# Chunked attention and a gated feed-forward on one core: q and k turned by the DMA crossbar from unit 8 on, and a new order around the first two blocks

## The chip, the core and the metric

The kernel runs on one core of a Trainium2 chip. The metric is device time in microseconds (us), the median of several executions. An execution has five engines that matter here: PE (TensorE: matmuls into PSUM), ACT (ScalarE), DVE (VectorE), POOL (GpSimd, which here issues loads and little else) and SP (SyncE, which issues stores and DMA transposes). DMAs that change the type are issued from POOL; every engine's own instructions run in the order in which the program emits them.

## The reference

```python
q, k, v: (8, 8, 576, 64) float32      # batch, heads, sequence, head size
# attention within chunks of 64 tokens, 9 chunks per sequence
scores = (1 / sqrt(64)) * q_c @ k_c^T           # 64 x 64 for a chunk and head
attn   = softmax(scores, axis=-1)
x      = (attn @ v_c)  -> (4608 tokens, 512)     # heads side by side
h      = x @ w_in                                # 512 -> 2048
g      = h * sigmoid(beta * h)
out    = g @ w_out                               # 2048 -> 512, float32
```

## The kernel before

All matmuls run in fp16 and sum in fp32. The 4608 tokens are cut into 18 **units** of 256 tokens (four chunks), and two units make a **block** of 512 tokens; there are nine blocks, `j` = 0 to 8.

A unit is attended in these steps, each a function that emits its instructions at once:

- `load_qk(u)`, `load_v(i)`: casting DMAs from POOL. Four units of q and k are held (`qk` pool, `bufs=4`); v stays as a whole. A partition of the q tile holds two neighbouring tokens, so a run of q in memory is 512 bytes.
- `emit_T(u)`: two DVE stream transposes (line 135) of k and q, on pairs of fp16 values taken as fp32 in 32 x 32 blocks. Head size lies then on 32 partitions, in an even and an odd half `e`. It ends with `loads_to(u + 4)`, which puts the loads of a unit four further on POOL's queue.
- `emit_sc(u)`: the scores (line 187), 64 matmuls with 32 rows and 64 columns of PE: 8 heads, 2 halves that accumulate, 4 chunks. ACT takes the exponential of all into `et` (line 196).
- `emit_pv(u)`: attention times v (line 208), 32 matmuls with 64 rows and 64 columns and 65 columns streamed; the 65th column, ones, gives the softmax's sum.
- `emit_norm(u, s)`: DVE's reciprocal and product, for one half (128 tokens) of the unit (lines 218, 220).
- the turn of x for the next matmul: `emit_xt_pe` (four PE transposes into `xp`, line 235, and a copy on ACT, line 237) in units 0 to 3 and 5, `emit_xt_dma` (a DMA transpose from SP, line 243) in the others.

The feed-forward of a block is `emit_m(j, m)` for 16 values of m (first layer: 4 matmuls at line 254 into `hps`, a tanh on ACT at line 262 and a product on DVE at line 263, which gives `gt`; it can run on half of the columns), and `emit_t(j, t)` for four groups of 128 tokens (second layer: 16 matmuls at line 276, a scaled copy `osb` on ACT at line 286 and a store from SP). Sigmoid is written through tanh, with the halves in `beta2` and in the last copy. `hps`, `ops`, `xp` and `warm` share four PSUM buffers; scores and one of the two PV results share one more (`ps_s`).

The order is written out by hand, and each engine keeps it. At the start, q and k of unit 0 come in two halves of four heads as fp32, four DMAs on SP's queue (line 301), and are cast by ACT (line 150) and DVE (line 151) in `emit_T_half`. Idle matmuls (`emit_idle`) stand between the steps. Then unit 1 is attended while the first layer of block 0 begins on its first 256 columns, and after it the second layer of block 0 runs, with the attention of unit 2 in it. For block 1 and later, each step gets a place between 0 and 1 in the block, and all are sorted by it: `m` and `h` (an `m` on columns 256 to 511) are first-layer steps of block j, `t` is a half of a second-layer group of block j - 1, and `att_items(u, a0, w)` places the attention of unit u from `a0` on over a width `w`:

```python
return [(a0, 2, ("sc", u)), (a0 + 0.40 * w, 3, ("pv", u)),
        (a0 + 0.41 * w, 3, ("norm", u, 0)), (a0 + 0.55 * w, 3, ("norm", u, 1)),
        (a0 + 0.70 * w, 3, ("T", u + 1))]
```

Block 1 (`j == 1`) has only first-layer steps, with the attention of unit 4 and the scores of unit 5 in it; the second layer of block 0 is over by then. From block 3 on, a block holds 16 first-layer steps, 8 second-layer halves and the attention of the two units of the next block.

Of the kernel before, what the change touches and what calls it, by code (L numbers as in the profile page):

```python
# [8 lines left out]
FP32 = mybir.dt.float32  # L9
# [6 lines left out]
def kernel(  # L16
# [10 lines left out]
    nc = tc.nc  # L27
# [27 lines left out]
    ident = const.tile([128, 128], FP16)  # L55
    idle = const.tile([128, 512], FP16)
    HH = H // 2
    raw0 = [[const.tile([128, HH, 2, D], FP32, name=f"raw{i}{a}") for i in range(2)] for a in range(2)]
    qk0 = [[const.tile([128, HH, 2, D], FP16, name=f"h0{i}{a}") for i in range(2)] for a in range(2)]
    qkT0 = [[const.tile([128, HH, CH, 2], FP16, name=f"t0{i}{a}") for i in range(2)] for a in range(2)]  # L60
    braw = const.tile([128, 32], FP32)
# [5 lines left out]

    blocks = [(u, 2) for u in range(0, NU, 2)]
    NB = len(blocks)
    unit_block = {}  # L70
    for j, (u0, n) in enumerate(blocks):
        for u in range(u0, u0 + n):
# [13 lines left out]
    def load_qk(u):  # L86
        for src, dst, nm in ((q, q_t, "qu"), (k, k_t, "ku")):
            t = qk_p.tile([128, H, 2, D], FP16, tag=nm, name=nm)
            for off, n, b, s in runs(u * UNIT, UNIT):
                nc.gpsimd.dma_start(  # L90
                    out=t[off // 2:(off + n) // 2],
                    in_=src[b, :, s:s + n, :].rearrange("h (p r) d -> p h r d", r=2),
                )
            dst[u] = t
# [35 lines left out]
    def emit_T(u, which=("kT", "qT")):  # L130
        for nm in which:
            src, dst = {"kT": (k_t, kT), "qT": (q_t, qT)}[nm]
            a = src.pop(u)
            t = qt_p.tile([128, H, CH, 2], FP16, tag=nm, name=nm)
            nc.vector.transpose(  # L135
                out=t.rearrange("p h s e -> p (h s e)").bitcast(FP32).rearrange(
                    "p (h i r) -> p h r i", h=H, r=2),
                in_=a.rearrange("p h r d -> p (h r d)").bitcast(FP32).rearrange(
                    "p (h r i) -> p h r i", h=H, r=2),
            )  # L140
            dst[u] = t
        loads_to(u + 4)

    et_t = {}
# [2 lines left out]
    xt_t = {}  # L147

    def emit_T_half(a):
        nc.scalar.copy(out=qk0[a][0], in_=raw0[a][0])  # L150
        nc.vector.tensor_copy(out=qk0[a][1], in_=raw0[a][1])
        for i in (0, 1):
            nc.vector.transpose(
                out=qkT0[a][i].rearrange("p h s e -> p (h s e)").bitcast(FP32).rearrange(
                    "p (h i r) -> p h r i", h=HH, r=2),
                in_=qk0[a][i].rearrange("p h r d -> p (h r d)").bitcast(FP32).rearrange(
                    "p (h r i) -> p h r i", h=HH, r=2),
            )
# [21 lines left out]
    def emit_sc(u, split=False):  # L180
        qt, kt = qT.pop(u), kT.pop(u)
        sc = ps_s.tile([128, 2, H, CH], FP32, tag="s", name="sc")
        for h in range(H):
            for e in range(2):
                for c in range(4):
                    p0, o0 = 32 * c, 64 * (c % 2)
                    nc.tensor.matmul(  # L187
                        out=sc[o0:o0 + 64, c // 2, h, :],
                        lhsT=kt[p0:p0 + 32, h, :, e],
                        rhs=qt[p0:p0 + 32, h, :, e],  # L190
                        start=(e == 0),
                        stop=(e == 1),
                    )
        et = et_p.tile([128, 2, H, CH], FP16, tag="et", name="et")
        for s in ([0, 1] if split else [slice(0, 2)]):
            nc.scalar.activation(out=et[:, s], in_=sc[:, s], func=ACTF.Exp, scale=scale)  # L196
        et_t[u] = et

    def emit_pv(u):
        et = et_t.pop(u)  # L200
        for s in range(2):
            i = 2 * u + s
            pool, tag = ((ps_x, "x"), (ps_s, "s"))[s]
            x = pool.tile([128, 2, 4, 128], FP32, tag=tag, name="x")
            for g in range(4):
                for r in range(2):
                    for c in range(2):
                        nc.tensor.matmul(  # L208
                            out=x[64 * c:64 * c + 64, r, g, 0:D + 1],
                            lhsT=et[64 * r:64 * r + 64, s, 4 * c + g, :],  # L210
                            rhs=vbig[64 * r:64 * r + 64, i, 4 * c + g, 0:D + 1],
                        )
            x_t[u, s] = x

    def emit_norm(u, s):
        x = x_t.pop((u, s))
        rd = rd_p.tile([128, 2, 4, 1], FP32, tag="rd", name="rd")
        nc.vector.reciprocal(out=rd, in_=x[:, :, :, D:D + 1])  # L218
        x16 = x_p.tile([128, 2, 4, D], FP16, tag="x16", name="x16")
        nc.vector.tensor_tensor(  # L220
            out=x16, in0=x[:, :, :, 0:D], in1=rd.to_broadcast([128, 2, 4, D]), op=ALU.mult
        )
        x16_t[u, s] = x16

    def xt_at(u, s):
# [5 lines left out]
    def emit_xt_pe(u, s, on_act=True):  # L231
        xf = x16_t.pop((u, s)).rearrange("p r h d -> p (r h d)")
        xp = ps_p.tile([128, 4, 128], FP16, tag="p", name="xp")
        for g in range(4):
            nc.tensor.transpose(out=xp[:, g, :], in_=xf[:, g * 128:(g + 1) * 128], identity=ident)  # L235
        if on_act:
            nc.scalar.copy(out=xt_at(u, s), in_=xp)  # L237
        else:
            nc.vector.tensor_copy(out=xt_at(u, s), in_=xp)

    def emit_xt_dma(u, s):
        xf = x16_t.pop((u, s)).rearrange("p r h d -> p (r h d)")
# [52 lines left out]
    with tc.manual_schedule():  # L295
        nc.vector.memset(idle, 0.0)
        nc.vector.memset(braw, 0.0)  # L297
        nc.vector.memset(vbig[:, :, :, D:D + 1], 1.0)
        for a in range(2):
            for i, src in enumerate((q, k)):  # L300
                nc.sync.dma_start(  # L301
                    out=raw0[a][i],
                    in_=src[0, HH * a:HH * a + HH, 0:UNIT, :].rearrange("h (p r) d -> p h r d", r=2),
                )
        bv = moe_beta.rearrange("(m w f) -> w m f", w=4, f=32)
# [52 lines left out]
        for s in range(4):  # L358
            for t in range(4):
                if s == 2 and t == 1:  # L360
                    emit_T(2)
                if s == 2 and t == 3:
                    emit_sc(2)
                if s == 3 and t == 0:
                    emit_pv(2)
                    emit_norm(2, 0)
                    emit_norm(2, 1)
                if s == 3 and t == 2:
                    emit_xt_pe(2, 0)
                    emit_xt_pe(2, 1)  # L370
                emit_t(0, t, 4 * s, 4 * s + 4)
        emit_T(3)
        emit_m(1, 0, 0, 256)
        emit_m(1, 1, 0, 256)
        emit_sc(3, True)
        for m in range(2, 5):
            emit_m(1, m, 0, 256)
        emit_pv(3)
        emit_norm(3, 0)
        emit_norm(3, 1)  # L380
        for m in range(5, 10):
            emit_m(1, m, 0, 256)
        emit_xt_pe(3, 0)
        emit_m(1, 10, 0, 256)
        emit_xt_pe(3, 1)

        def att_items(u, a0, w):
            return [(a0, 2, ("sc", u)), (a0 + 0.40 * w, 3, ("pv", u)),
                    (a0 + 0.41 * w, 3, ("norm", u, 0)), (a0 + 0.55 * w, 3, ("norm", u, 1)),
                    (a0 + 0.70 * w, 3, ("T", u + 1))]  # L390

        for j in range(1, NB):
            items = []
            if j == 1:
                items += [(0.04 * m, 0, ("h", m)) for m in range(11)]
                items += [(0.44 + 0.11 * (m - 11), 0, ("m", m)) for m in range(11, KFF)]
                items += [(0.05, 3, ("T", 4)), (0.25, 2, ("sc", 4)), (0.42, 3, ("pv", 4)),
                          (0.43, 3, ("norm", 4, 0)), (0.50, 3, ("norm", 4, 1)), (0.58, 3, ("T", 5)),
                          (0.85, 3, ("sc", 5))]
            else:  # L400
                m0 = 0.27 if j == 2 else 0.02
                items += [(m0 + (1 - m0) * m / KFF, 0, ("m", m)) for m in range(KFF)]
                for t in range(4):
                    for hf in range(2):
                        items.append((0.98 * (t + 0.5 * hf) / 4, 1, ("t", t, hf)))
                if j == 2:
                    items += [(0.01, 3, ("pv", 5)), (0.02, 3, ("norm", 5, 0)), (0.06, 3, ("norm", 5, 1)),
                              (0.13, 3, ("xp", 5, 0)), (0.19, 3, ("xp", 5, 1)), (0.20, 3, ("T", 6))]
                if j + 1 < NB:
                    if j == 2:  # L410
                        items += att_items(6, 0.32, 0.34) + att_items(7, 0.66, 0.30)
                    else:
                        for i in range(2):
                            items += att_items(2 * j + 2 + i, 0.03 + 0.43 * i, 0.43)
            items.sort(key=lambda it: it[:2])
            for _, _, it in items:
# [68 lines left out]
```

## Time and profile before

| | |
|---|---|
| time, median of 4 runs | 300.25 us (299.41 to 301.15) |
| the profiled execution | 300.13 us |
| its span, first to last instruction | 298.4 us |
| mean granted TensorE clock | 0.988 |
| PE, DVE, ACT busy | 282.4, 152.1, 148.5 us |
| PE alone on the chain that ended last | 88% |
| DMA transposes, casting loads of q, k, v | 26 of 128 x 512 fp16; 68, most of 128 or 256 KB as written |

The span is what the profile shows of one execution, and the time of that execution is 1.7 us longer. "Busy" is the union of an engine's instructions; a busy PE need not be a PE at its peak. A view by stage tells more than the totals: the same engine can be full in one stage and waiting in another. Times within the profile are counted from the span's start. "Landing" of a DMA is counted from its issue.

### The profile page before, as it was taken

To read this page: it belongs to the slowest core of one execution; us is meant where nothing else is said; L and a number is where in the kernel's file an instruction comes from. 1 tells how busy PE (TensorE), PEld (TensorE's weight loads), DVE (VectorE), ACT (ScalarE), POOL (GpSimd) and SP (SyncE) were. 2 spreads that over 40 slices of the span, in tenths; PEclk is the share of its full clock that TensorE was granted. 3 is DMA by queue.
4 is the path that set the end of the run, shared out by engine and by line. 5 is a ranking of instruction groups with operands and counts; after the bars stand their busy time and mean duration, and the time that the engine had idled before them with its cause. 6 is when DMAs were issued, how large, how long until landed. Compare 5 with 4: busy or idle time off the path is not lost.

```text
span 298.4 us, 7145 instructions
## 1 busy us (share of the span) xinstructions
PE 282.4 (95%) x3046; PEld 142.1 (48%) x3046; DVE 152.1 (51%) x278; ACT 148.5 (50%) x232; POOL 78.9 (26%) x104
## 2 busy tenths in 40 slices
PE   6679999787999999999999999999999999999995
PEld 2555445663544444444444444444444444444444
DVE  2557514787446738373737373737273736443300
ACT  3278417774645555445544554545555454544411
POOL 8663478384406041431153104000000000000000
PEclk9599999999999999999999999999999999999999
DMA  8999999999986992939292929211120112100011
GB/s 151 180 194 204 163 178 208 210 165 161 164 99 100 130 141 74 142 76 140 73 139 76 142 64 147 73 37 51 57 73 28 47 57 74 45 37 35 35 73 71
DMA packets 101136, 32.20 MB, mean 108 GB/s; under 512 B 88176, under 2 KB 96624, under 8 KB 101104
## 3 DMA queue, kind: packets, MB, share of 16 engines
q0 software_dynamic: 79392, 17.83, 65.5%
q1 hardware_dynamic: 21568, 13.78, 15.5%
q8 instruction: 24, 0.39, 0.5%
q10 hardware_dynamic: 144, 0.13, 0.1%
q14 instruction: 8, 0.07, 0.1%
HBM read 36.71 MB, written 9.44 MB: 155 GB/s over the span
## 4 chain that ended last, share of the span: by engine, by line
PE 88%; DVE 5%; DMA 2%; ACT 2%; issue 1%; SPq 0%; DVEq 0%; ACTq 0%
PE ops L276 41%; PE hps L254 39%; PE sc L187 4%; DMA raw<-in_k_dram 2%; PE x L208 2%; DVE gt L263 2%; DVE x L220 1%; PE ops L440 1%; ACT xt L237 1%; ACT sg L262 1%; DVE kT L135 1%; DVE qT L135 1%; PE xp L235 1%; SPq L301 0%; ACT et L196 0%
## 5 line engine op out<-in xcount | busy, mean ns | idle before, releaser
L263 DVE SCALAR_TENSOR_TENSOR gt<-sg,hps 128x512 f16<-128x512 f32 (+1 forms) x161 | 100.0, 627 | 111.0 <-ACT sg L262 110.2
L262 ACT ACTIVATE sg<-hps,beta 128x512 f32<-128x512 f32 (+1 forms) x161 | 102.3, 643 | 78.2 <-PE hps L254 76.0
L254 PE MATMUL hps<-xt,win 128*128 128x512 f16 (+1 forms) x644 | 138.1, 357 | 3.2 <-DVE gt L263 1.9
L276 PE MATMUL ops<-wout,gt 128*128 128x512 f16 x560 | 130.9, 379 | 0.0
L254 PEld LDWEIGHTS <-win 128*128 128x128 f16 x644 | 60.8, 98 | 61.3 <-issue 3.8
L276 PEld LDWEIGHTS <-gt 128*128 128x128 f16 x560 | 54.0, 98 | 63.8
L286 ACT ACTIVATE osb<-ops 128x512 f32<-128x512 f32 x35 | 20.9, 597 | 42.1 <-PE ops L276 42.1
L90 POOL DMA_DIRECT2D qu<-in_q_dram x23 | 18.0, 789 | 82.9 <-DVE qT L135 80.7
L98 POOL DMA_DIRECT2D vbig<-in_v_dram x40 | 34.1, 868 | 10.9 <-DMA wout<-in_moe_w_out_dram 3.8
L220 DVE TENSOR_TENSOR x<-x,rd 128x512 f16<-128x512 f32 x36 | 24.9, 691 | 1.2
L196 ACT ACTIVATE et<-sc 128x1024 f16<-128x1024 f32 (+1 forms) x19 | 17.5, 933 | 12.1 <-PE sc L187 12.1
L90 POOL DMA_DIRECT2D ku<-in_k_dram x23 | 18.1, 790 | 2.7 <-DMA win<-in_moe_w_in_dram 2.2
L187 PEld LDWEIGHTS <-kT 32*64 32x64 f16 x1088 | 10.2, 106 | 8.7 <-DVE qT L135 5.3
L187 PE MATMUL sc<-qT,kT 32*64 32x64 f16 x1088 | 12.1, 192 | 2.1 <-DVE qT L135 2.1
L135 DVE STREAM_TRANSPOSE kT<-ku 128x512 f32<-128x512 f32 x17 | 12.0, 705 | 2.2 <-DMA ku<-in_k_dram 2.2
L218 DVE RECIPROCAL rd<-x 128x8 f32<-128x8 f32 x36 | 7.2, 200 | 9.0 <-PE x L208 9.0
L135 DVE STREAM_TRANSPOSE qT<-qu 128x512 f32<-128x512 f32 x17 | 11.4, 670 | 0.0
L208 PEld LDWEIGHTS <-et 64*64 64x64 f16 x576 | 6.4, 109 | 7.0 <-issue 3.4
L293 PE MATMUL warm<-idle 128*128 128x128 f16 (+1 forms) x42 | 7.5, 350 | 1.2 <-DVE braw L297 1.2
L208 PE MATMUL x<-vbig,et 64*64 64x65 f16 x576 | 8.4, 197 | 0.2 <-ACT et L196 0.2
L237 ACT COPY xt<-xp 128x512 f16<-128x512 f16 x10 | 5.7, 587 | 3.4 <-PE xp L235 3.3
L453 DVE TENSOR_SCALAR osb<-ops 128x256 f32<-128x256 f32 x1 | 0.4, 425 | 12.5 <-PE ops L440 12.5
(26 smaller groups left out, 37.7 us busy)
## 6 DMA issues: line engine op xcount, KB each, us to landing
out_dram<-osb SPq DMA_DIRECT2D x35, 256.0 KB, 2.2
vbig<-in_v_dram POOLq DMA_DIRECT2D x32, 128.0 KB, 5.9
qu<-in_q_dram POOLq DMA_DIRECT2D x11, 256.0 KB, 5.3
ku<-in_k_dram POOLq DMA_DIRECT2D x11, 256.0 KB, 5.9
win<-in_moe_w_in_dram POOLq DMA_DIRECT2D x8, 256.0 KB, 9.7
wout<-in_moe_w_out_dram POOLq DMA_DIRECT2D x4, 512.0 KB, 13.1
qu<-in_q_dram POOLq DMA_DIRECT2D x4, 192.0 KB, 7.9
ku<-in_k_dram POOLq DMA_DIRECT2D x4, 192.0 KB, 8.0
```

The source lines that it names most:

```text
L90: nc.gpsimd.dma_start(out=t[off // 2:(off + n) // 2], in_=src[b, :, s:s + n, :].rearrange("h (p r) d -> p h r d", r=2),)
L98: nc.gpsimd.dma_start(out=vbig[off:off + n, i, :, 0:D], in_=v[b, :, s:s + n, :].rearrange("h p d -> p h d"),)
L135: nc.vector.transpose(out=t.rearrange("p h s e -> p (h s e)").bitcast(FP32).rearrange("p (h i r) -> p h r i", h=H, r=2), in_=a.rearrange(" ...
L187: nc.tensor.matmul(out=sc[o0:o0 + 64, c // 2, h, :], lhsT=kt[p0:p0 + 32, h, :, e], rhs=qt[p0:p0 + 32, h, :, e], start=(e == 0), stop=(e == 1),
L196: nc.scalar.activation(out=et[:, s], in_=sc[:, s], func=ACTF.Exp, scale=scale)
L208: nc.tensor.matmul(out=x[64 * c:64 * c + 64, r, g, 0:D + 1], lhsT=et[64 * r:64 * r + 64, s, 4 * c + g, :], rhs=vbig[64 * r:64 * r + 64, i, ...
L220: nc.vector.tensor_tensor(out=x16, in0=x[:, :, :, 0:D], in1=rd.to_broadcast([128, 2, 4, D]), op=ALU.mult)
L254: nc.tensor.matmul(out=hps[:, 0:n], lhsT=w_in16[m // 2][:, kk, (m % 2) * 128:(m % 2) * 128 + 128], rhs=xr[:, c0 // CH:(c0 + n) // CH, 2 * ...
L262: nc.scalar.activation(out=sg[:, 0:n], in_=hps[:, 0:n], func=ACTF.Tanh, scale=beta2[:, m:m + 1])
L263: nc.vector.scalar_tensor_tensor(out=gt_t[j][:, m, c0:c0 + n], in0=sg[:, 0:n], scalar=1.0, in1=hps[:, 0:n], op0=ALU.add, op1=ALU.mult,)
L276: nc.tensor.matmul(out=ops, lhsT=gt_t[j][:, kk, t * 128:(t + 1) * 128], rhs=w_out16[kk // 4][:, kk % 4, :], start=(kk == 0), stop=(kk == K ...
L286: nc.scalar.activation(out=osb, in_=ops, func=ACTF.Copy, scale=0.5)
```

## The change

It has five parts.

1. **Start.** Heads 4 to 7 of the first q and k are loaded by two casting DMAs from POOL, ahead of the loads of v, straight into the fp16 tiles; the casts of that half go away. In `emit_T_half` the transpose of q comes before the cast of k.
2. **Norm and turn of units 0 and 1.** DVE's product runs in two halves in units 0 and 1, and the copy of the turned x in two halves in unit 0.
3. **Units 8 to 17 (`XU = 8`).** q and k are loaded token by token, one token to a partition, so runs are 256 bytes in memory and 128 as written, and there are twice as many DMAs. `emit_T` becomes two DMA transposes from SP of 128 x 1024 fp16. The scores become 32 matmuls with 64 rows and 64 columns, without accumulation. `emit_pv` reads `et` in the new order. T of such a unit stands at 0.10 w of the unit before, instead of 0.70 w.
4. **Before block 1.** T(3) is emitted after norm(2), within the second layer of block 0, and sc(3) right after that layer, ahead of the first-layer steps; 8 instead of 11 steps of block 1 run on the first 256 columns.
5. **Blocks 1 and 2.** sc(4) to norm(4), T(5), sc(5) move from block 1 to the head of block 2, where second-layer halves of block 1 run; T(4) moves to 0.80 of block 1. Unit 4's x is now turned by PE and ACT, as unit 5's. The first layer of block 2 starts at 0.30 instead of 0.27 and units 6 and 7 a little later.

```diff
-    raw0 = [[const.tile([128, HH, 2, D], FP32, name=f"raw{i}{a}") for i in range(2)] for a in range(2)]
+    raw0 = [const.tile([128, HH, 2, D], FP32, name=f"raw{i}") for i in range(2)]
...
+    XU = 8
...
     def load_qk(u):
         for src, dst, nm in ((q, q_t, "qu"), (k, k_t, "ku")):
             t = qk_p.tile([128, H, 2, D], FP16, tag=nm, name=nm)
+            if u >= XU:
+                dst[u] = t
+                tv = t.rearrange("p h r d -> p (h r d)").rearrange("p (s h d) -> p s h d", s=2, h=H)
+                for sp in range(2):
+                    for off, n, b, s in runs(u * UNIT + sp * 128, 128):
+                        nc.gpsimd.dma_start(
+                            out=tv[off:off + n, sp],
+                            in_=src[b, :, s:s + n, :].rearrange("h p d -> p h d"),
+                        )
+                continue
...
     def emit_T(u, which=("kT", "qT")):
...
+            if u >= XU:
+                nc.sync.dma_start_transpose(
+                    out=t.rearrange("p h s e -> p (h s e)").rearrange("p (j t) -> p j t", t=128),
+                    in_=a.rearrange("p h r d -> p (h r d)"),
+                )
+                continue
...
     def emit_T_half(a):
-        nc.scalar.copy(out=qk0[a][0], in_=raw0[a][0])
-        nc.vector.tensor_copy(out=qk0[a][1], in_=raw0[a][1])
+        if a == 0:
+            nc.scalar.copy(out=qk0[a][0], in_=raw0[0])
         for i in (0, 1):
+            if a == 0 and i == 1:
+                nc.vector.tensor_copy(out=qk0[a][1], in_=raw0[1])
...
     def emit_sc(u, split=False):
...
+        if u >= XU:
+            qx, kx = (t.rearrange("p h s e -> p (h s e)").rearrange("p (j c t) -> p j c t", j=H, c=2)
+                      for t in (qt, kt))
+            for jj in range(H):
+                for par in range(2):
+                    for c in range(2):
+                        nc.tensor.matmul(
+                            out=sc[64 * c:64 * c + 64, par, jj, :],
+                            lhsT=kx[64 * par:64 * par + 64, jj, c, :],
+                            rhs=qx[64 * par:64 * par + 64, jj, c, :],
+                        )
...
     def emit_norm(u, s):
...
+        for r in ([0, 1] if u < 2 else [slice(0, 2)]):
+            o = x16[:, r]
+            nc.vector.tensor_tensor(
+                out=o, in0=x[:, r, :, 0:D], in1=rd[:, r].to_broadcast(list(o.shape)), op=ALU.mult
+            )
...
     def emit_xt_pe(u, s):
...
         for g in range(4):
             nc.tensor.transpose(out=xp[:, g, :], in_=xf[:, g * 128:(g + 1) * 128], identity=ident)
+            if u == 0 and g % 2:
+                nc.scalar.copy(out=xt[:, g - 1:g + 1], in_=xp[:, g - 1:g + 1])
+        if u:
+            nc.scalar.copy(out=xt, in_=xp)
...
-        for a in range(2):
+        for a, eng, dst in ((0, nc.sync, raw0), (1, nc.gpsimd, qk0[1])):
             for i, src in enumerate((q, k)):
-                nc.sync.dma_start(
-                    out=raw0[a][i],
+                eng.dma_start(
+                    out=dst[i],
...
                     emit_norm(2, 1)
+                    emit_T(3)
...
-        emit_T(3)
-        emit_m(1, 0, 0, 256)
-        emit_m(1, 1, 0, 256)
         emit_sc(3, True)
-        for m in range(2, 5):
+        for m in range(3):
             emit_m(1, m, 0, 256)
         emit_pv(3)
         emit_norm(3, 0)
         emit_norm(3, 1)
-        for m in range(5, 10):
+        for m in range(3, 6):
             emit_m(1, m, 0, 256)
         emit_xt_pe(3, 0)
-        emit_m(1, 10, 0, 256)
+        emit_m(1, 6, 0, 256)
         emit_xt_pe(3, 1)
+        emit_m(1, 7, 0, 256)
...
-                    (a0 + 0.70 * w, 3, ("T", u + 1))]
+                    (a0 + (0.70 if u + 1 < XU else 0.10) * w, 3, ("T", u + 1))]
...
-                items += [(0.04 * m, 0, ("h", m)) for m in range(11)]
-                items += [(0.44 + 0.11 * (m - 11), 0, ("m", m)) for m in range(11, KFF)]
-                items += [(0.05, 3, ("T", 4)), (0.25, 2, ("sc", 4)), (0.42, 3, ("pv", 4)),
-                          (0.43, 3, ("norm", 4, 0)), (0.50, 3, ("norm", 4, 1)), (0.58, 3, ("T", 5)),
-                          (0.85, 3, ("sc", 5))]
+                items += [(0.04 * m, 0, ("h", m)) for m in range(8)]
+                items += [(0.32 + 0.085 * (m - 8), 0, ("m", m)) for m in range(8, KFF)]
+                items += [(0.80, 3, ("T", 4))]
...
-                m0 = 0.27 if j == 2 else 0.02
+                m0 = 0.30 if j == 2 else 0.02
...
-                    items += [(0.01, 3, ("pv", 5)), (0.02, 3, ("norm", 5, 0)), (0.06, 3, ("norm", 5, 1)),
-                              (0.13, 3, ("xp", 5, 0)), (0.19, 3, ("xp", 5, 1)), (0.20, 3, ("T", 6))]
+                    items += [(0.00, 0, ("sc", 4)), (0.05, 3, ("pv", 4)), (0.06, 3, ("norm", 4, 0)),
+                              (0.07, 3, ("norm", 4, 1)), (0.08, 3, ("T", 5)), (0.13, 2, ("sc", 5)),
+                              (0.16, 2, ("xp", 4, 0)), (0.18, 2, ("xp", 4, 1)), (0.20, 2, ("pv", 5)),
+                              (0.21, 3, ("norm", 5, 0)), (0.22, 3, ("norm", 5, 1)), (0.23, 3, ("T", 6)),
+                              (0.27, 2, ("xp", 5, 0)), (0.29, 2, ("xp", 5, 1))]
...
-                        items += att_items(6, 0.32, 0.34) + att_items(7, 0.66, 0.30)
+                        items += att_items(6, 0.36, 0.32) + att_items(7, 0.68, 0.29)
...
-                    if it[1] != 5:
+                    if it[1] not in (4, 5):
                         emit_xt_dma(it[1], it[2])
```

More of the change, by code (lines that the diff above doesn't have):

```diff
@@ L134, in emit_T @@
             t = qt_p.tile([128, H, CH, 2], FP16, tag=nm, name=nm)
+            dst[u] = t
+            if u >= XU:
[4 more added lines that the diff above has]
+                continue
             nc.vector.transpose(
@@ L140, in emit_T @@
             )
-            dst[u] = t
         loads_to(u + 4)
@@ L182, in emit_sc @@
         sc = ps_s.tile([128, 2, H, CH], FP32, tag="s", name="sc")
+        if u >= XU:
[9 more added lines that the diff above has]
+                        )
+            et = et_p.tile([128, 2, H, CH], FP16, tag="et", name="et")
+            nc.scalar.activation(out=et, in_=sc, func=ACTF.Exp, scale=scale)
+            et_t[u] = et
+            return
         for h in range(H):
@@ L209, in emit_pv @@
                             out=x[64 * c:64 * c + 64, r, g, 0:D + 1],
-                            lhsT=et[64 * r:64 * r + 64, s, 4 * c + g, :],
+                            lhsT=(et[64 * r:64 * r + 64, s, 4 * c + g, :] if u < XU else
+                                  et[64 * r:64 * r + 64, g % 2, 4 * s + 2 * c + g // 2, :]),
                             rhs=vbig[64 * r:64 * r + 64, i, 4 * c + g, 0:D + 1],
@@ L219, in emit_norm @@
         x16 = x_p.tile([128, 2, 4, D], FP16, tag="x16", name="x16")
-        nc.vector.tensor_tensor(
-            out=x16, in0=x[:, :, :, 0:D], in1=rd.to_broadcast([128, 2, 4, D]), op=ALU.mult
-        )
+        for r in ([0, 1] if u < 2 else [slice(0, 2)]):
[3 more added lines that the diff above has]
+            )
         x16_t[u, s] = x16
@@ L229, in xt_at, with emit_xt_pe @@
         return xt_t[j][:, 2 * o + s]
-    def emit_xt_pe(u, s, on_act=True):
+    def emit_xt_pe(u, s):
         xf = x16_t.pop((u, s)).rearrange("p r h d -> p (r h d)")
         xp = ps_p.tile([128, 4, 128], FP16, tag="p", name="xp")
+        xt = xt_at(u, s)
         for g in range(4):
             nc.tensor.transpose(out=xp[:, g, :], in_=xf[:, g * 128:(g + 1) * 128], identity=ident)
[L236 to L239, printed above, removed]
+            if u == 0 and g % 2:
+                nc.scalar.copy(out=xt[:, g - 1:g + 1], in_=xp[:, g - 1:g + 1])
+        if u:
+            nc.scalar.copy(out=xt, in_=xp)
     def emit_xt_dma(u, s):
```

## The prediction

> **What bounds the kernel now.** First the page, for the engine that is busy and for how long:
>
> ```profile
> span 298.4 us, 7145 instructions
> ...
> PE 282.4 (95%) x3046; PEld 142.1 (48%) x3046; DVE 152.1 (51%) x278; ACT 148.5 (50%) x232; POOL 78.9 (26%) x104
> ...
> PE   6679999787999999999999999999999999999995
> ```
>
> TensorE is full from about 75 us to the end; only the first ten slices have room. Then one row per stage from the windows view (columns: length, then busy time of PE, PEld, DVE, ACT and POOL, the granted clock, the DMA share, GB/s):
>
> ```profile
> 49.34:58.10 8.76, 6.64 (x149) 5.41 (x147) 5.76 (x15) 7.16 (x16) 4.07 (x7) 1.00 1.70 235
> 58.10:71.94 13.84, 11.48 (x225) 7.62 (x225) 10.61 (x23) 9.32 (x17) 8.67 (x11) 1.00 1.99 165
> 71.94:102.95 31.01, 31.01 (x361) 14.76 (x360) 17.65 (x32) 16.23 (x25) 10.51 (x14) 1.00 1.12 124
> 102.95:133.03 30.08, 30.08 (x322) 14.08 (x320) 17.19 (x31) 15.31 (x22) 9.37 (x12) 1.00 0.82 109
> ```
>
> The reader is to see that block 1 (49 to 72 us) leaves PE idle 2.1 + 2.4 us, and that from block 2 on it is never idle: there only removed PE work counts. Last the chain of waits, for the rates of PE work and for the start:
>
> ```profile
> 2.34 6.75 DMA raw<-in_k_dram
> ...
> 14.23 0.62 DVE kT L135
> ...
> 69.61 0.61 DVE qT L135
> 70.26 0.71 PE sc L187 x64
> ...
> 104.68 0.86 PE hps L254 x4
> 105.54 0.64 PE sc L187 x64
> 106.18 0.97 PE hps L254 x4
> ...
> 109.74 0.38 PE x L208 x32
> ```
>
> In the full stretch a unit's scores (64 matmuls of 32x64) take 0.64 us, its PV (32 of 64x64x65) 0.38 us, a first-layer step of 512 columns 0.86 (of 256: 0.43), a second-layer half 1.73, and each change of tile shape 0.10 (0.97 against 0.86).
>
> **Scores in 64x64 tiles, units 8 to 17.** 64 matmuls become 32, without accumulation. The trace has no such score, but its neighbour in form, PV, has the same tiles, the same rotation over them and one column more: 0.38. Ends: 0.32 (at the 10 ns a piece of today's scores) and 0.64 (nothing gained). I take 0.38, so 10 x 0.26 = 2.6 us less on a full PE (0 to 3.2). Shape changes are as many as before.
>
> **Crossbar for q and k of these units.** DVE loses 20 transposes of 0.70 and 0.67 us, worth nothing: DVE is 57% busy in a full block. SP gets two DMA transposes per unit, each of twice today's size. The rows:
>
> ```profile
> xt<-x SPq DMA_TRANSPOSE x26, 2.3
> ...
> 99.60 2.62 SPq L243 DMA_TRANSPOSE xt<-x  x2
> ```
>
> Two of today's hold SP 2.62 us, so two double ones some 4.8 us, and they should land about 6 us after the first issue; beside a load burst today's took 5.8 (issues at 66.7 to 69) instead of 2.3, so up to 10. They are issued at a0 + 0.10 w and wanted at the next unit's sc: (0.43 - 0.043) x 30.08 = 11.6 us later. That cover hides them. Queued behind them on SP are the stores and the xt transposes of the same unit. A store waits at most 4.8 us, and four osb buffers of some 7 us each cover that. The second xt of a block, issued at 0.70 of it, now meets the load burst that follows T: up to 6.5 us instead of 2.3, with 9 us until the next block's first layer. Cost 0; without cover, each us late is a us of PE.
>
> The loads: POOL issues four q/k pieces of v's form instead of two per unit. Here a rule speaks against the change. The row: in the burst issued from 104.1 to 106.8, q lands after 4.3 us, k after 5.5, the two v pieces (rows of half the length) after 5.4 each, thus 0.87 apart, as they are issued. The Trainium skill ("DMA: Bandwidth & Descriptors", Specifications) puts line rate at 512 B and says that less makes the engine read, modify and write. By the row the burst of 8.0 us (104.18 to 112.2) grows by two issues to 9.8 of the 15.0 us that a unit lasts. If shorter rows doubled the 2.0 us between q's and k's landing, it would be 12, still under 15. Neither changes the sum; the second eats into T's cover.
>
> Moved with these: T(4), from 0.05 to 0.80 of block 1, issues the loads of unit 8 on POOL later, by some 8 us; they are wanted by T(8) at about 95 us, 20 us after. T(8) and later stand 0.6 w earlier than before, which only releases POOL's loads sooner. At the start the four beta loads stand behind two pieces on SP instead of four: sooner. DVE's order in half 0 (q's transpose before k's cast) delays sc by at most 0.3 us under warm-up work: 0.
>
> **The start.** Half 1 of the first q, k goes to POOL's queue as fp16. Gone are 0.59 us of cast on DVE, one on ACT, and 512 KB on SP's queue. Two pieces of 128 KB issued together at 118 us landed after 3.6 us (median); issued at 1.25 and about 2.1, after POOL's v pieces no longer come first, k is there at 6 to 7 instead of 9.09. What is late next: v moves behind them (two issues, 1.6 us), PV(0) to about 8.6 instead of 12.0; norm(0), with its halves at 0.42 (a 256-wide DVE row) instead of one 0.69, ends near 11.2; then ku of unit 1. It lands now at 3.98 + 8.8 = 12.8. The bytes ahead of it are half as many to write, so I put it at 11.8 (11.2 to 12.8). kT starts at 11.85 instead of 14.23: 2.4 us. Off that: 0.3 for the split norm(1), which is on the chain; and 0.7 for what comes late then, the weights: win group 1 lands at 7.93 + 9.2 = 17.1 and its first matmul starts at 17.66, so more than 0.5 us is gained only as far as that load comes earlier too.
>
> The clock is the second place for a rule:
>
> ```profile
> 8.00:9.00 1.00, 0.00 (x0) 0.00 (x0) 0.00 (x0) 0.20 (x1) 0.98 (x2) 0.50 1.93 176
> ...
> 14.00:15.00 1.00, 0.99 (x13) 0.82 (x10) 1.00 (x3) 0.52 (x1) 0.64 (x1) 0.74 1.99 191
> ```
>
> Half clock lasts from before 8 to about 14.5 us and is over when the first layer starts at 16.2. The skill ("TensorE: Matmul & The Clock Gate", Part 1) says that a free-running window of about 3.4 us with an idle PE halves the clock, and one busy window restores it. By the row alone the shorter wait at 7 to 10 us avoids the half clock: cost 0. By the rule PE, which now waits from about 11.5 to 13.2, can enter the first layer cold, and 1.9 us of work in such a window doubles. PE waits there anyway, so I take 0.3. The start gives 2.4 - 0.3 - 0.7 - 0.3 = 1.1 us (0.3 to 2.6).
>
> **Block 1 and the head of block 2.** Today the end of T(0) to the first ops of block 2 (49.34 to 71.94) is 22.6 us. The new order, by the same rows, from 0 = 49.34:
> - T(3): on DVE it already starts at 46.33, straight after norm(2); its load comes late on POOL, which runs behind until 59. The move is worth 0. sc(3) comes first: 0 to 0.64, its exp (two halves, 1.08) to 1.85, so pv(3) follows m0 to m2 at 2.04 unhindered. But norm(3) comes behind three gt on DVE and ends at 5.2; xp(3,0) waits 0.6 for it, m6 about 0.95 for the PSUM that gt(3) frees behind norm, h0 0.45 for ACT's copy. h0 starts at 7.2 with 2.0 us idle; today at 8.76 after three more steps of 0.43: 0.3 gained.
> - Eight h and eight m, nearly back to back: PE ends m15 at 17.7. T(4) stands behind gt(13) on DVE, and from that gt's start to sc it took 1.95 us before (68.31 to 70.26), so sc(4) starts at 18.65: 0.95 idle.
> - In the head of block 2 PE runs in order: sc(4), t, pv(4), t, sc(5). From pv to the end of qT took 3.36 us (44.26 to 47.62) and one t covers 1.8: idle 1.2. pv(5) waits for exp(5) (1.08 and latencies) under xp(4) alone, 0.5: idle 0.7. m0 waits for two ACT copies behind xp(5): 1.05. ACT's and DVE's other work there is light.
> - sc(4), sc(5), pv(4), xp(4) on PE with three shape changes: 0.64 + 0.64 + 0.38 + 0.45 + 0.3 = 2.4.
>
> That is 18.65 + 2.4 + 2.95 = 24.0 against 22.6: the overlap is bought with waits of its own, and xp(4) is extra. Loss 1.4 us (0.3 to 2.8). The tighter first layers of block 2 (m0 at 0.30) keep ACT under PE: 16 x 0.69 + 3.8 us in 25.
>
> **Sum.** 300.13 (the profiled execution; 0.12 under the median of 300.25) - 2.6 - 1.1 + 1.4 = 297.8; against the median 297.9.
>
> **Rivals.**
> - The forecast: faster by 1.5 us or more, centre 297.9. A measurement of this kernel tells about 0.5% (1.5 us) from nothing. Chance 0.60.
> - Start bound by weights, middle at its bad end: 0.3 - 2.8 + 2.6 = +0.1 gained, about 300.0. For it: DMA is full until 36 us. Against: half 1 is no longer written as fp32. Chance 0.28.
> - Slower: the crossbar pair lands late. For it: SP's queue is in order, and 5.8 instead of 2.3 us beside a burst. Against: the next burst is only released when T has landed. It decides from 11.6 us after issue; break-even is 0.24 us beyond; at 12.3 us ten score blocks wait 0.7 each, 7 - 2.3 = 4.7 us slower, 304.9. Chance 0.12.
> - That it doesn't do what it says: the 64x64 tiles don't overlap. PV's 0.38 speaks against it; without that gain 300.5, counted in the second case.
>
> The range of 8 in 10 leaves out the far tail of the third and the best ends of all terms: 295.8 to 300.3.
>
> **What would show it.** Right: sc of 0.35 to 0.40 us x32 and blocks of 29.5 us instead of 30.08; kT of unit 1 near 11.9 us; PE waits of 0.9 to 1.2 us at sc(4), sc(5) and m0 of block 2. Wrong: sc waiting for a DMA transpose in full blocks; win waited for at 16 to 18 us; half clock past 15 us; or block 1 and 2 together shorter than today's 53.6 us.

## The result and the profile after

The changed kernel takes 299.57 us in the median (43 executions), the kernel before 300.18 (62 executions): ratio 0.9958, 95% interval 0.9945 to 0.9970, a gain of 0.42%. The ratio, here and below, leaves out executions more than 1.5% above the fastest of the same kernel (11 of the 43, none of the 62), while medians and ranges keep them: the median of all 43 is only 0.2% below the one before. The forecast was 297.9, and 0.6 of its chance lay on more than 0.5%; the direction held and the size fell short by half. Single executions of the changed kernel range from 296.9 to 306.0 us, those of the kernel before from 299.0 to 301.2. The profiled execution took 298.58 us, 1.55 less than the one profiled before.

From the page, the head and the row of PE, with DMA's row that belongs to it now:

```profile
span 296.8 us, 6545 instructions
...
PE   6679998887899979999999999999999999999995
...
PEclk9999999999999999999999999999999999999999
DMA  9999999999996999999999999464527312100111
```

PE has a new dent at about 105 us (the 7 in the fifteenth slice), and DMA is full until about 185 us but for one slice at 89 to 96 us. The half clock at 8 to 14 us is gone in this execution. The stages from the windows view (columns as before: length, busy time of PE, PEld, DVE, ACT, POOL, clock, DMA share, GB/s):

```profile
47.64:66.80 19.16, 16.73 (x265) 11.23 (x266) 14.03 (x30) 15.07 (x29) 8.63 (x13) 1.00 1.69 182
66.80:102.50 35.70, 33.04 (x469) 16.15 (x466) 20.06 (x38) 18.71 (x27) 22.49 (x27) 1.00 1.71 129
102.50:132.10 29.60, 28.08 (x250) 12.67 (x249) 14.02 (x24) 13.82 (x20) 12.71 (x15) 1.00 1.88 159
132.10:161.65 29.55, 29.55 (x257) 13.53 (x256) 14.04 (x24) 15.11 (x22) 12.39 (x16) 1.00 1.52 140
```

A full block lasts 29.55 us instead of 30.08, but block 3 (the third row) leaves PE idle for 1.5 us. While loads last, the DMA share of a full block went from 0.82 to 1.52 in block 4 and 1.43 in block 5. The chain of waits names the idle time:

```profile
11.59 0.71 DVE kT L153
...
99.24 6.06 DMA xt<-x
105.30 0.54 issue
105.84 1.02 PE hps L292 x4
106.86 0.38 PE sc L208 x32
107.24 0.97 PE hps L292 x4
```

The new score block takes 0.38 us. In front of it the first layer of block 3 waits for the DMA transpose of x of unit 7, which landed 6.06 us after its issue at 99.24 (the second, issued at 100.67, landed after 5.07). PE's waits, from the waits view (total us, times, longest):

```profile
PE sc L221 <- DVE qT L153: 3.3, 3, 1.2
PE hps L292 <- ACT xt L277: 2.2, 4, 0.9
PE hps L292 <- DMA xt<-x: 1.5, 1, 1.5
```

The third line has no counterpart in the kernel before. Summed from chain to chain: start 1.70 us less (the first layer runs unbroken from 19.87 instead of 21.57), blocks 1 and 2 1.33 more (54.94 instead of 53.61 from the end of T(0) to block 3), the wait 1.52 more, five full blocks 5 x 0.53 = 2.65 less: 1.50 less, where the span shows 1.6.

### The profile page after: what moved, and what is told of

It reads as the page before. It is cut to its first block, busy times and chain, and to the rows that moved or that the text cites. A ratio compares the mean times of both kernels' runs of the same rounds, so it can differ in the third digit from the quotient of the medians.

```text
span 296.8 us, 6545 instructions
## 1 busy us (share of the span) xinstructions
PE 280.0 (94%) x2722; PEld 137.5 (46%) x2722; DVE 140.8 (47%) x258; ACT 148.2 (50%) x232; POOL 97.1 (33%) x124
## 4 chain that ended last, share of the span: by engine, by line
PE 85%; DVE 4%; DMA 4%; ACT 3%; issue 1%; POOL 1%; DVEq 0%; ACTq 0%; POOLq 0%
PE hps L292 39%; PE ops L314 39%; DMA xt<-x 2%; DMA ku<-in_k_dram 2%; PE x L242 2%; PE sc L221 2%; DVE x L257 1%; PE sc L208 1%; PE ops L478 1%; ACT xt L277 1%; ACT et L230 1%; ACT sg L300 1%; DVE gt L301 1%; DVE kT L153 1%; DVE qT L153 1%
## 5 line engine op out<-in xcount | busy, mean ns | idle before, releaser
L95 POOL DMA_DIRECT2D qu<-in_q_dram x22 | 18.6, 853 | 62.2 <-DMA qT<-qu 47.3
L257 DVE TENSOR_TENSOR x<-x,rd 128x512 f16<-128x512 f32 (+1 forms) x40 | 25.1, 637 | 1.2
L95 POOL DMA_DIRECT2D ku<-in_k_dram x22 | 18.8, 875 | 0.0
L230 ACT ACTIVATE et<-sc 128x1024 f16<-128x1024 f32 (+1 forms) x9 | 7.3, 833 | 13.4 <-PE sc L221 13.3
L214 ACT ACTIVATE et<-sc 128x1024 f16<-128x1024 f32 x10 | 10.2, 1016 | 0.0
L101 POOL DMA_DIRECT2D qu<-in_q_dram x10 | 7.8, 786 | 2.0 <-DMA win<-in_moe_w_in_dram 1.6
L101 POOL DMA_DIRECT2D ku<-in_k_dram x10 | 7.7, 771 | 2.1 <-DMA win<-in_moe_w_in_dram 1.3
L221 PE MATMUL sc<-qT,kT 32*64 32x64 f16 x448 | 5.0, 192 | 3.3 <-DVE qT L153 3.3
L331 PE MATMUL warm<-idle 128*128 128x128 f16 (+1 forms) x42 | 6.6, 310 | 1.2 <-DVE braw L335 1.2
L221 PEld LDWEIGHTS <-kT 32*64 32x64 f16 x448 | 4.3, 106 | 6.0 <-DVE qT L153 3.4
L153 DVE STREAM_TRANSPOSE kT<-ku 128x512 f32<-128x512 f32 x7 | 4.9, 706 | 3.6 <-DMA ku<-in_k_dram 3.6
```

What stands on the lines that cost most here:

```text
L95: nc.gpsimd.dma_start(out=tv[off:off + n, sp], in_=src[b, :, s:s + n, :].rearrange("h p d -> p h d"),)
L101: nc.gpsimd.dma_start(out=t[off // 2:(off + n) // 2], in_=src[b, :, s:s + n, :].rearrange("h (p r) d -> p h r d", r=2),)
L153: nc.vector.transpose(out=t.rearrange("p h s e -> p (h s e)").bitcast(FP32).rearrange("p (h i r) -> p h r i", h=H, r=2), in_=a.rearrange(" ...
L221: nc.tensor.matmul(out=sc[o0:o0 + 64, c // 2, h, :], lhsT=kt[p0:p0 + 32, h, :, e], rhs=qt[p0:p0 + 32, h, :, e], start=(e == 0), stop=(e == 1),
L257: nc.vector.tensor_tensor(out=o, in0=x[:, r, :, 0:D], in1=rd[:, r].to_broadcast(list(o.shape)), op=ALU.mult)
```

## The experiments

All times are medians; the ratio is to the kernel before on the same chip, whose median was 299.8 to 300.4 us in these sets. A trace is of one execution each.

### One part undone at a time

No crossbar and no 64x64 scores:

```diff
-    XU = 8
+    XU = 18
```

> Crossbar and 64x64 scores left out (every unit takes the old path); new start and new middle kept. Theory A (the three parts add: start -1.7 us, middle +1.3, scores -2.6, wait for x of unit 7 +1.5): 300.2 - 1.7 + 1.3 = 299.8 us, PE never waits in the full blocks, block 3's first m0 starts without a wait, and single runs lie within about 2 us as those of the kernel before. Rival B (the wait of 1.5 us at block 3 comes from the later place of unit 7 in block 2, not from the crossbar): the wait for xt stays, 301.3 us. Rival C (the wide scatter of the changed kernel, 296.9 to 306, comes from the new start or middle): scatter stays 4 us or more.

Measured: 300.61 us, ratio 1.0017 (0.9999 to 1.0035), executions from 299.35 to 301.95. No PE wait for xt. So the scatter and the wait come with the crossbar part, not with the later place of unit 7, which stayed. But the level is 0.8 us above Theory A's sum, while its profiled execution has a span of only 297.4: something in start or middle costs more in most executions than in the profiled one. It is taken up below, under the clock.

Parts 4 and 5 undone:

```diff
-            items += [(0.80, 3, ("T", 4))]
+            items += [(0.05, 3, ("T", 4)), (0.25, 2, ("sc", 4)), ... (0.85, 3, ("sc", 5))]
...
-                    items += [(0.00, 0, ("sc", 4)), (0.05, 3, ("pv", 4)), ...
+                    items += [(0.01, 3, ("pv", 5)), (0.02, 3, ("norm", 5, 0)), ...
```

> Parts 4 and 5 undone (order before block 1, in block 1 and at the head of block 2 as before); new start and crossbar kept. Theory A: 300.2 - 1.7 - 2.6 = 295.9 us plus a wait for x of unit 7 of 0 to 2 us at block 3, so 296 to 298, faster than the changed kernel by 1.3 us. Rival B (the new order of the middle is worth what it costs, since T(4), T(5) and the crossbar loads need it): no faster than the changed kernel, 298.5 or more, with new waits in block 1 that the old order did not have.

Measured: 298.33 us, ratio 0.9926 (0.9899 to 0.9953), executions from 296.31 to 306.66. Faster than the whole change by about 1 us, as Theory A has it, though the two intervals just touch: the new middle costs. The scatter stays.

Parts 1 and 2 undone:

```diff
-        for a, eng, dst in ((0, nc.sync, raw0), (1, nc.gpsimd, qk0[1])):
+        for a in range(2):
             for i, src in enumerate((q, k)):
-                eng.dma_start(
-                    out=dst[i],
+                nc.sync.dma_start(
+                    out=raw0[a][i],
```

> Parts 1 and 2 undone (four fp32 loads on SP, whole products and copies); crossbar and new middle kept. Theory A: kT of unit 1 back at 14.2 us, first full-rate layer step at 21.6 us, half clock between about 8 and 14.5 us back; 298.6 + 1.7 = 300.3 us for an execution like the profiled one, 301 in the median. Rival (the start's gain is given back where weights or loads come late): difference under 0.7 us.

Measured: 301.74 us, ratio 1.0034 (1.0011 to 1.0057). The difference to the whole change is 0.0076 of 300, 2.3 us, where the rival allowed 0.7. The half clock is back in its profile (9.4 to 16.2 us). Its waits for xt differ too, 1.9 us at block 3 and another of 1.3 at block 5, so not all of the 2.3 us belongs to the start.

### Without the transpose that block 3 waited for

```diff
-                    if it[1] not in (4, 5):
+                    if it[1] not in (4, 5, 7):
...
+                        items += [(0.92, 2, ("xp", 7, 0)), (0.95, 2, ("xp", 7, 1))]
```

> The changed kernel with x of unit 7 turned by PE and ACT instead of two DMA transposes. Theory A (block 3 waits 1.5 us for these two transposes, which land 5 to 6 us after issue because the crossbar and the loads of unit 11 are in flight): the wait goes, eight PE transposes and two shape changes cost 0.55, so 1 us faster than the changed kernel, 297.6 in an execution like the profiled one. Rival (the scatter has its source in the full blocks): same scatter, waits of a us or more in later blocks, mean gain under 0.5 us.

Measured: 305.09 us, ratio 1.0139 (1.0098 to 1.0181): Theory A fell. The wait at block 3 is gone, and blocks 4 and 5 wait instead (2.8 and 1.5 us). Its x transposes from 96 to 190 us, from the view of that tile (ns that an issue takes, first and last issue, and then the time to landing):

```profile
L281 SPq DMA_TRANSPOSE xt<-x x10: 1188/1190/1211, 114.8 to 182.5; - x10
DMA to landing us min/median/max: 4.0/6.2/8.4
```

So no single transpose was at fault: from block 4 on they are late here as a rule, and with the wait at block 3 gone later blocks wait. And two waits were followed by a window at half clock (rows of its windows view):

```profile
74.00:77.00 3.00, 3.00 (x8) 1.05 (x9) 2.72 (x6) 0.34 (x1) 3.00 (x4) 0.50 2.26 179
...
138.00:142.00 4.00, 3.35 (x39) 1.34 (x40) 0.69 (x1) 1.45 (x2) 0.00 (x0) 0.57 0.95 199
```

The first follows the waits at the head of block 2, the second the wait for xt at block 4.

### What makes x late

Three kernels take the crossbar part apart. In the first, DVE turns q and k, while loads, scores and the early place of T stay:

```diff
-            if u >= XU:
-                nc.sync.dma_start_transpose(...)
-                continue
             nc.vector.transpose(
```

> Units 8 to 17 turn q and k by DVE's stream transposes instead of the crossbar; token-wise loads and 64x64 scores stay. The layout is then not what the scores expect, so only the times count. Theory M (crossbar transposes and casting loads of short rows, in flight together, hold each other up; x of the odd unit lands late and PE waits at the first layer of blocks 3 to 5): no wait for xt, full blocks of 29.55 us from block 3 on, 300.6 (the kernel without crossbar) - 2.6 = 298.0 us, single runs within 3 us. Rival L (the doubled number of short loads alone is too much for the DMA engines): waits for xt stay, median as the changed kernel's 299.6 and scatter of 5 us or more.

Measured: 303.05 us, ratio 1.0079 (1.0046 to 1.0112), executions from 300.57 to 305.12. Theory M fell as the only cause: without any transpose of q or k, x is as late, and block 3 waits 3.0 us for it. In the second, the crossbar stays and the loads are those of before:

```diff
-            if u >= XU:
+            if u >= 18:
                 dst[u] = t
```

> Crossbar and 64x64 scores stay for units 8 to 17, but q and k of these units are loaded in the old form (two tokens to a partition, runs of 512 bytes read and 256 written, half as many). The layout is then not what the crossbar expects, so only the times count. Theory M: transposes still meet loads, so late landings and waits for xt stay, perhaps fewer since the burst is some 1.7 us shorter: 298.5 to 300 us with scatter. Rival L (short rows at fault): waits and scatter go, 298.0 us. Theory S (SP's queue, held by the pair of transposes for 4 to 5 us, delays x's issue): issue times of xt as in the changed kernel and waits stay.

Measured: 300.98 us, ratio 1.0013 (0.9983 to 1.0043), executions from 297.61 to 304.61, and three blocks wait for xt, 3.3 us in all. The doubled number of short rows is not needed for it either. What both share with the changed kernel is T's place at 0.10 w. With DVE turning as in the first, and T back at its old place:

```diff
-                    (a0 + (0.70 if u + 1 < XU else 0.10) * w, 3, ("T", u + 1))]
+                    (a0 + 0.70 * w, 3, ("T", u + 1))]
```

> As the kernel that turns q and k of units 8 to 17 on DVE with token-wise loads and 64x64 scores (layout not what the scores expect, only the times count), with T back at 0.70 w of the unit before instead of 0.10 w. Theory P (not the crossbar pair but the place of T counts: T releases the loads of the unit four further, and at 0.10 w this burst runs while x of the odd unit goes through the crossbar): bursts again follow x's transposes, these land within 3 us, no wait for xt at blocks 3 to 5; 600 ns to 3 us less per block start than with T early, about 298.0 to 299 us instead of 303.0. Rival L (the doubled number of short loads is at fault wherever it stands): waits for xt stay, 301 us or more.

Measured: 298.18 us, ratio 0.9933 (0.9908 to 0.9958), executions from 297.02 to 298.80, no wait for xt. One number moved and 4.9 us went (0.0146 between the ratios, as the two ran on different chips). The x transposes of the two, T early and then T late:

```profile
L275 SPq DMA_TRANSPOSE xt<-x x12: 1188/1196/1207, 100.7 to 180.5; - x12
DMA to landing us min/median/max: 2.8/5.3/7.9
```

```profile
L275 SPq DMA_TRANSPOSE xt<-x x14: 1188/1196/1206, 99.1 to 187.1; - x14
DMA to landing us min/median/max: 2.3/2.3/2.6
```

Between these two kernels T's place is the only difference, so here it is the cause. T frees the q and k buffers and so releases the loads of the unit four further. With T early, the next burst starts at 100.09 us, just ahead of x of unit 7; with T late, x is through before it starts at 103.70. First T early, then T late, from the timelines of POOL and SP:

```profile
100.09 1.83 POOL L95 DMA_DIRECT2D qu<-in_q_dram  x2
100.71 2.63 SPq L275 DMA_TRANSPOSE xt<-x  x2
```

```profile
99.12 2.63 SPq L275 DMA_TRANSPOSE xt<-x  x2
103.70 1.77 POOL L95 DMA_DIRECT2D qu<-in_q_dram  x2 [5.13 <-DVE qT L147]
```

With the crossbar, the same early place delays x of unit 7 in another way. The changed kernel issues its loads at 91.95 to 98.7 us, as the kernel with T late does (91.83 to 98.6), and the burst that T(8) releases starts only at 103.50, when x should have landed. What is new is T(8) itself: its pair of transposes is issued at 92.17 and 93.73, into those loads. Of the transfers issued from 91.9 to 98.8 us in the changed kernel, a load and the pair, and then the same load in the kernel with T late (count, KB each, median us to landing):

```profile
ku<-in_k_dram POOLq DMA_DIRECT2D x2, 64.0 KB, 7.2
kT<-ku SPq DMA_TRANSPOSE x1, 7.3
qT<-qu SPq DMA_TRANSPOSE x1, 9.2
```

```profile
ku<-in_k_dram POOLq DMA_DIRECT2D x2, 64.0 KB, 3.6
```

So in block 3 of the changed kernel it is Theory M's collision, pair and loads in flight together, with x behind them, and T's place put the pair there. No run moved a crossbar T(8) alone, so this part is read from traces; the last version below, with T(8) on DVE and late, agrees with it.

### The clock

The kernel without crossbar, with idle matmuls where PE waits at the head of block 2:

```diff
             for _, _, it in items:
+                if j == 2 and it in (("sc", 4), ("sc", 5), ("pv", 5), ("m", 0)):
+                    emit_idle({"sc": 12, "pv": 6, "m": 12}[it[0]], 128)
```

> The kernel without crossbar and 64x64 scores (XU = 18), new start and new middle, with idle matmuls in front of sc(4), sc(5), pv(5) and the first m of block 2, where PE waits 3.6 us in sum within 11 us. Clock theory (these waits halve the clock for a window of 3.4 us in many executions, which costs up to 1.7 us on a PE that is otherwise full, and this is why the median of 300.6 lies above the profiled 299.2): 299.3 to 299.8 us and less scatter. Rival (the head of block 2 costs only its waits): 300.6 us or slower by the overrun of the filler, some 0.3.

Measured: 299.94 us, ratio 1.0001 (0.9986 to 1.0015), against 1.0017 (0.9999 to 1.0035) without the filler; executions from 299.22 to 300.48 instead of 299.35 to 301.95. The mean granted clock of the 12 executions rose from 0.993 to 0.997, and the median moved as the clock theory says, 0.67 us; yet the intervals overlap, so the gain in time is made likely and not settled. The narrower range is plain.

### Versions

Crossbar only for the last four units, whose T comes when the loads are over, with the old middle; then the same with filler at the start:

```diff
-    XU = 8
+    XU = 14
```

> XU = 14 instead of 8 (crossbar and 64x64 scores only for units 14 to 17, whose transposes run when the last loads are over), and parts 4 and 5 undone. Theory M: no transpose of q or k meets a burst of loads, so no wait for xt; gain 4 x 0.26 = 1.05 for scores, 1.7 for the start, none for the middle: about 297.5 us, scatter of 3 us. Rival (late xt come from SP's queue or from the 128 x 1024 transposes themselves): waits of 1 us or more remain in blocks 5 to 7.

Measured: 297.73 us, ratio 0.9926 (0.9897 to 0.9955), executions from 297.12 to 298.81, no wait for xt.

```diff
-        emit_idle(8, 128)
+        emit_idle(16, 128)
         emit_T_half(1)
...
         emit_xt_pe(0, 1)
+        emit_idle(16, 128)
         emit_T(1)
```

> As the kernel with XU = 14 and the old middle, with 8 more idle matmuls after the first half's scores and 16 more before T(1), in stretches in which PE waits for q and k. Clock theory (a window of 3.4 us at half clock comes in most executions from PE's waits at the start and costs up to 1.7 us when it falls on the first layer): mean granted clock 0.998 or more and 0.5 to 1 us faster than without the filler, smaller scatter. Rival (the start is bound by the loads of k of unit 1 and of the weights, whatever the clock): same within 0.4 us, or slower by what the filler overruns.

Measured: 297.40 us, ratio 0.9908 (0.9880 to 0.9936), executions from 297.08 to 297.71; mean clock 0.999 in its profile instead of 0.994. All six executions had a clock of 0.998 or more, where four of the seven without filler had 0.994. The gain of 0.3 us is within the intervals; the range shrank from 1.7 to 0.6 us.

Crossbar from unit 8 again, with T of the even units behind a store:

```diff
-                    (a0 + (0.70 if u + 1 < XU else 0.10) * w, 3, ("T", u + 1))]
+                    (a0 + (0.70 if u + 1 < XU else 0.37 if u % 2 and u > XU else 0.10) * w, 3, ("T", u + 1))]
```

> Crossbar from unit 8 on, old middle, new start with filler; T of the even units from 10 on is placed at 0.37 instead of 0.10 of the odd unit before, behind the store of the third second-layer group, so that the burst of loads which it releases comes after x of the odd unit. Theory P: x of the odd unit lands within 3 to 4 us of its issue, no wait for xt from block 4 on, 297.4 - 1.55 (six more units with the short scores) = 295.9 us with a scatter of 2 us. Rival (the pair of transposes on the same queue ahead of x is enough to make it late, since SP works 4.8 us on it): x is issued 2 to 3 us later than before and PE waits about 1 us at each block: 298 to 301 us.

Measured: 299.28 us, ratio 0.9985 (0.9958 to 1.0012), executions from 297.40 to 301.01. From block 4 on x of the odd unit lands in 2.3 to 2.9 us and no block waits, although the pair stands right ahead of it (in block 4 kT at 125.14, qT at 127.42, x at 128.76): the loads before have landed and the next are released later. So a pair ahead of x on the queue is not enough to make it late. But block 3 waits 2.4 us: T(8) had kept its early place in this kernel, with its pair at 90.54 and 91.92 beside the loads issued from 90.32. With T(8) and T(9) on DVE at 0.70, and every crossbar T of an even unit at 0.37:

```diff
-    XU = 8
+    XU = 10
...
+                    (a0 + (0.70 if u + 1 < XU else 0.37 if u % 2 else 0.10) * w, 3, ("T", u + 1))]
```

> As the kernel with the later T of even units, but crossbar and 64x64 scores from unit 10 on: T(8) and T(9) run on DVE at 0.70, so that no pair of transposes and no burst stands before x of unit 7. Theory P: the wait of 2.4 us at block 3 goes and no other comes, so 297.4 (XU = 14 with filler) - 4 x 0.26 = 296.4 us with a scatter of about 1 us. Rival (block 3's wait only moves on to a later block): 297.5 us or more, with a wait for xt at block 4 or 5 and a scatter of 3 us.

Measured: 296.37 us, ratio 0.9867 (0.9847 to 0.9887), executions from 296.14 to 296.93. This is the fastest of all, 1.3% under the kernel before, and where Theory P put it. Several parts differ from the change here, so the 1.3% is that of the whole. Its block 3, from the windows view:

```profile
102.42:132.00 29.58, 29.58 (x319) 13.84 (x318) 15.60 (x28) 14.81 (x23) 12.96 (x15) 1.00 1.17 124
```

## Why the prediction was right and where it was wrong

- **Scores, 0.38 us and 2.6 us in sum.** Right: 0.38 from the neighbour in form, full blocks of 29.55 us, 5 x 0.53 = 2.65.
- **Start, 1.1 us.** Right in its steps: k's half is there for the transpose at 6.95 us, kT of unit 1 starts at 11.59 (11.85 said), win is waited for 1.0 us at 16.7. The sum measured 1.70. The clock term, 0.3 us for a cold first layer, did not come up in the profiled execution (clock 1.00 throughout). It is real in others: half clock lies between 13.07 and 16.48 us in the profile with the old middle. The rule that the prediction quoted speaks of an idle PE; there PE had been busy for 1.23 of the 3.41 us before, so it need not be idle.
- **Head of block 2, a loss of 1.4 us.** Right, and nearly wait by wait: 0.95 at sc(4) against 0.99, 1.2 at sc(5) against 1.14, 0.7 at pv(5) against 0.59, 1.05 at m0 against 0.94 (forecast first); 1.33 us in sum against 1.4. What was missing is that waits so dense can halve the clock: rows of 0.50 and 0.57 at 74 to 78 us stand in the traces of two of the experiments.
- **"With 9 us until the next block's first layer. Cost 0."** This step failed. It took the place 0.70 in the sorted list for a time, 0.3 of a block before the next one. The trace of before had the time:

```profile
127.58 2.62 SPq L243 DMA_TRANSPOSE xt<-x  x2
```

  The second of these is issued at 129.0 and the first layer that needs it starts at 134.8, so the cover was 5.7 us; in block 2 it was 3.6 (issued at 101.0, needed at 104.7), 1.3 more than a landing of 2.3. The landing of "up to 6.5 us" was foreseen, and with the right cover it is a wait of up to 3 us. Measured: 1.5 us in the profiled execution, in the traces of the experiments up to 3.0 us, and in other blocks too.
- **The third rival, a late crossbar.** Half right. Its mechanism, transposes beside a load burst, is what cost the time; but PE waited for x, not for the pair of q and k. The pair's case was close: in the first seven of its ten units it landed 8.8 to 10.9 us after its first issue, with a cover put at 11.6; in the last three, without loads, 4.5 to 6.2, as forecast. The argument against this rival, that the next burst is only released when T has landed, held (103.50 after 102.98), but overlooked the burst that the T before had released.
- **Loads of short rows.** The row read rightly: 9.8 us for a burst of six loads was forecast, and without the pair (DVE turning, T late) the one from 103.70 us takes 9.45. The price of shorter rows, 12 us, did not show there. In the changed kernel the burst from 103.50 takes 13.0, with the pairs and x in flight beside it; that term was missing, and how it divides is open.
- **The second rival, 300.0 us**, came nearest to the median in number, not by its mechanism: weights cost 1.0 us and the middle its expected 1.3. That the median lies inside the forecast's range at all owes something to luck: the start gained 0.6 us more than said, which made up for part of a wait that was put at nothing.
- **Median against profile.** The profiled execution (298.58) lies 1 us under the median of 299.57. Late x and half clock differ between the traces, and the clock between executions. Sorted by their mean granted clock, the 43 executions have medians of 297.8 us (11 at 0.997 or more), 299.5 (19 at 0.993 or 0.994) and 300.8 (13 at 0.992 or less); a forecast from one profile does not hold this term. How often x is late can't be told, as only one execution of each kernel has its trace.

## What to carry to other kernels

A step that frees a buffer also fires a load: when it is moved, look at what the load will then run beside, and read the cover of that transfer off the trace's issue and need, never off a place in a written order. A wait on a full engine costs more than its length where it brings the clock down. A kernel that scatters over 9 us where the one before scattered over 2 is worth more than one trace. A new transfer form is to be placed where its neighbours on the queues are quiet; here XU = 10 with T behind a store, the old middle and filler gained 1.3% where the change gained 0.42%.

## What the hardware showed beyond that

Half clock begins and ends on a grid of 3.41 us in these traces: it lasts 3.41 us, or twice that at the start of the kernel before (7.69 to 14.52). So the window in front of a change can be looked at. First the kernel before, then the one turned by DVE with T early, with its window at half clock:

```profile
4.28:7.69 3.41, 1.75 (x44) 0.91 (x42) 1.35 (x3) 0.72 (x3) 3.34 (x5) 1.00 1.31 180
```

```profile
70.83:74.24 3.41, 1.85 (x105) 1.50 (x106) 1.12 (x3) 2.13 (x4) 3.19 (x5) 1.00 2.14 188
74.24:77.65 3.41, 3.41 (x12) 1.46 (x11) 2.71 (x5) 0.33 (x1) 3.41 (x5) 0.50 2.26 158
```

PE was busy for 51% and 54% of these windows, and half clock followed; no idle window is needed. But the busy share alone doesn't decide. In the changed kernel 59% (2.00 us, 11.80 to 15.21) was followed by full clock, and so was 46% in the kernel with the old start, at its wait for x:

```profile
104.98:108.39 3.41, 1.58 (x8) 0.49 (x6) 1.12 (x2) 0.58 (x1) 1.84 (x3) 1.00 1.76 216
108.39:111.80 3.41, 3.33 (x46) 1.59 (x47) 0.74 (x2) 2.18 (x3) 3.41 (x4) 1.00 1.65 208
```

What decides beside it was not tried. So short waits close together may halve the clock of a PE that is busy half of the time, and these traces give no share from which on it is safe.
